# A three-stage attention and mixture kernel: the first mixture in blocks of 768 tokens, routing logits on TensorE, three token lists

## The chip, the core and the metric

The kernel runs on one core of a Trainium2 chip. Its engines work from queues of their own and meet through semaphores: TensorE multiplies (a weight load and a matmul each), VectorE and ScalarE read the accumulators in PSUM, GpSimd works on SBUF and issues the indirect DMAs, SyncE (SP) issues all other DMAs. The metric is the device time of one execution in microseconds (us), the median of several.

## The reference

What is computed, cut to its core (B=4, H=8, S=576, D=64, so 2304 tokens of 512 features; 8 experts, 1024 hidden features; float32 throughout):

```python
def phi(x):
    proj = np.einsum('bhsd,df->bhsf', x, w_phi)
    proj = proj - np.max(np.abs(proj), axis=-1, keepdims=True)
    return np.concatenate([np.exp(proj), np.exp(-proj)], axis=-1)
kv = einsum('bhsf,bhsd->bhfd', phi(k), v); z = sum(phi(k), axis=2)
x = einsum('bhsf,bhfd->bhsd', phi(q), kv) / (einsum('bhsf,bhf->bhs', phi(q), z)[..., None] + 1e-06)
# first mixture: every expert on every token, weighted by a Sinkhorn-normalised gate
P = np.exp(x @ w_gate - (x @ w_gate).max())
for _ in range(8):
    P /= P.sum(1, keepdims=True) + 1e-09
    P /= P.sum(0, keepdims=True) + 1e-09
    P *= N / E
x = sum(P[:, e:e + 1] * (np.maximum(x @ w1[e], 0.0) @ w2[e]) for e in range(E))
# second mixture: each token to the expert with the largest cosine logit
logits = (x / norm(x)) @ (emb / norm(emb)).T / tau
e = argmax(logits, axis=1); gate = softmax(logits)[e]
out[t] = gate[t] * (np.maximum(x[t] @ w1b[e[t]], 0.0) @ w2b[e[t]])
```

## The kernel before

Matrices are multiplied as float32r with a correction: each operand is split into a high part (a rounding copy, on ScalarE) and a low part (the difference, on VectorE or GpSimd), and each product is three matmuls, high by high, high by low, low by high.

**Attention** takes eight units (two batches by two heads), each in five chunks of keys and five of queries. Its output goes, transposed, to the DRAM tensor xd. While it runs, a background queue (`bg`) prepares the first expert's weights and the first block's activations, one task a step.

**First mixture.** The tokens are cut into four blocks of 512 and one of 256 (`BLOCKS`). For each expert and block there are two halves g of the hidden features. A half's first layer (`p1_group`) is a Winograd-Strassen scheme on 2 x 2 parts of the features and the tokens: seven products instead of eight, each of 12 matmuls of 256 columns, with adds on VectorE between them; `halves` then makes the relu's high part on ScalarE and its low part on VectorE. The 256-token block takes four plain products. The second layer (`p2_tile`) takes each tile of 128 tokens through 12 matmuls of 512 columns, and VectorE adds the result, weighted by the gate Pm, to an accumulator (acca, accb). Weights arrive in tiles called raw and go through `w1_tasks` (sums and splits, 11 operations a half, shared by VectorE and GpSimd) and `w2_task`. The block's activations are loaded again from xd in every step (`xload`), and their sums and splits made again (`x_tasks`, `xpiece`), by GpSimd and ScalarE.

The order is written out by hand: the instruction order of each engine is the order of the calls. `at_tick(step, g, i, fn)` puts a task behind a place of a step: the products of a half are its first ticks, the tiles of its second layer the next ones. `hooks` holds generators, of which one piece is issued at chosen ticks: `gate_logits` (gate products of a block, then the transposes) and `sinkhorn`, whose rounds alternate between VectorE and a matmul with ones (L676).

**Routing.** When the accumulators of a block are done, the second mixture's logits are made. For the first twelve tiles `dot_v` multiplies and sums a tile with an expert's embedding on VectorE (L749, four experts), `dot_p` and `dot_s` on GpSimd and ScalarE (the other four); for the last six `route_a` transposes a tile on TensorE and `route_l` multiplies it with the embeddings. `route_b` to `route_d` find each token's expert and its place in the expert's list with small VectorE operations and two matmuls; `route_w` writes the rows to the DRAM tensor x2d; `route_i` scatters the token numbers of one tile into the DRAM list ids with an indirect DMA, one tile after another into the same tensor:

```python
    def route_i(t0, i):
        si = rt[t0]["si"]
        G.indirect_dma_start(out=ids, out_offset=bass.IndirectOffsetOnAxis(si[:, i:i + 1], 0), in_=tokid[:, t0 + i:t0 + i + 1], in_offset=None)
```

**Second mixture.** 22 blocks of 128 list entries (25 if the counts need it), each of one expert. The first five (`NEARLY`) come from the first twelve tiles alone, so that they can start before the rest is routed. For each: `load_ids` reads the list, `gather` fetches the rows (tile xg), `tx` transposes them, `p1` and `p2` are the two layers, `th_` transposes the hidden rows in between; `wcond` loads an expert's weights when the expert changes, `wsplit` splits them. The output rows are scattered to their tokens.

## Time and profile before

| | |
|---|---|
| median of 3 runs | 2157.77 us (2156.74 to 2158.98) |
| the profiled execution's own time | 2161.89 us |
| its span, first to last instruction | 2160.0 us |
| mean granted TensorE clock | 0.979 |
| busy: TensorE, VectorE, ScalarE, GpSimd | 2052.9, 1289.6, 852.0, 886.1 us |
| moved by DMA | 148.78 MB, 69 GB/s in the mean |

The profile is of one execution, so durations and places below are of that one. Busy time of TensorE counts a matmul from its issue to its modelled end; consecutive matmuls overlap, so what one costs in a row of them is the distance of their starts, not its duration.

### The profile page before, as it was taken

The page shows a single profiled execution, that of the slowest core. Times are in us where ns is not written, and L with a number is a line of the kernel's source. Part 1 is how long each engine was busy: PE and PEld are TensorE (multiplying, and loading weights), DVE is VectorE, ACT ScalarE, POOL GpSimd, SP SyncE. Part 2 cuts the span into 40 slices and gives each one's busy share as a digit, 9 for nine tenths or more (in the row PEclk, how much of TensorE's full clock was granted, in tenths as well). Part 3 has the DMA queues.
Part 4 walks back from the last instruction along what each step waited for, and adds up shares of the span by engine and source line. Part 5 has one row for each costly group of instructions (what it writes and reads, how often), then busy time and mean ns, then how long its engine had stood idle before and what let it go on. Part 6 is the DMA issues. An engine that isn't in the chain of part 4 may idle for free.

```text
span 2160.0 us, 33113 instructions
## 1 busy us (share of the span) xinstructions
PE 2052.9 (95%) x12937; PEld 1839.7 (85%) x12937; DVE 1289.6 (60%) x1951; ACT 852.0 (39%) x1514; POOL 886.1 (41%) x678
## 2 busy tenths in 40 slices
PE   9999999999999999999999999999998886689997
PEld 8999889789989988898989899899987775568886
DVE  6776532764464464447446544744568784499996
ACT  5666422332342232224223222422334442468875
POOL 1234423343362344426224443532467662134442
PEclk9999999999999999999999999999999997889999
DMA  3443200111030012002100300310121013442851
GB/s 107 128 135 91 85 11 30 60 58 40 11 115 23 20 52 77 20 30 98 40 20 30 98 20 30 95 43 20 40 88 33 27 30 70 82 153 82 309 193 61
DMA packets 70674, 148.78 MB, mean 69 GB/s; under 512 B 10464, under 2 KB 30176, under 8 KB 70514
## 3 DMA queue, kind: packets, MB, share of 16 engines
q1 hardware_dynamic: 66418, 136.12, 19.8%
q0 software_dynamic: 4096, 10.51, 1.7%
q8 instruction: 103, 1.69, 0.3%
q14 instruction: 57, 0.47, 0.1%
HBM read 186.86 MB, written 15.32 MB: 94 GB/s over the span
## 4 chain that ended last, share of the span: by engine, by line
PE 67%; DVE 13%; issue 8%; DMA 5%; ACT 4%; POOL 3%; SPq 1%; POOLq 0%; DVEq 0%; ACTq 0%
PE psD L692 10%; PE psD L693 10%; PE psD L691 9%; PE psA L465 9%; PE psA L467 9%; PE psA L466 9%; PE psD L203 3%; DMA ids<-tokid,si 2%; DVE psB L749 2%; DMA xg<-x2d,idt 2%; DVE s2l L984 1%; PE psB L174 1%; DVE s1l L984 1%; PE psC L174 1%; DVE h1l L475 1%
## 5 line engine op out<-in xcount | busy, mean ns | idle before, releaser
L402 POOL TENSOR_TENSOR xlB<-xr,xhB 128x512 fp32r<-128x512 f32 x112 | 147.9, 1321 | 581.0 <-ACT xhB L401 578.8
L707 DVE SCALAR_TENSOR_TENSOR acca<-psD,Pm,acca 128x512 f32<-128x512 f32 x224 | 167.7, 749 | 237.6 <-PE psD L693 235.8
L691 PE MATMUL psD<-w2h,h1h 128*128 128x512 f32 x576 | 226.6, 393 | 7.6 <-ACT h1h L474 7.6
L691 PE MATMUL psD<-w2h,h0h 128*128 128x512 f32 x576 | 228.3, 396 | 3.1 <-DVE acca L707 3.1
L692 PE MATMUL psD<-w2h,h1l 128*128 128x512 f32 x576 | 227.0, 394 | 3.0 <-DVE h1l L475 3.0
L692 PE MATMUL psD<-w2h,h0l 128*128 128x512 f32 x576 | 225.7, 392 | 1.5 <-DVE h0l L475 1.4
L693 PE MATMUL psD<-w2l,h0h 128*128 128x512 f32 x576 | 226.3, 393 | 0.0
L693 PE MATMUL psD<-w2l,h1h 128*128 128x512 f32 x576 | 225.1, 391 | 0.1
L465 PE MATMUL psA<-xhT,wS 128*128 128x256 f32 x768 | 215.4, 280 | 0.0
L467 PE MATMUL psA<-xhT,wS 128*128 128x256 f32 x768 | 214.3, 279 | 0.0
L466 PE MATMUL psA<-xlT,wS 128*128 128x256 f32 x768 | 214.3, 279 | 0.0
L466 PE MATMUL psA<-xlB,wA 128*128 128x256 f32 x640 | 179.4, 280 | 4.1 <-POOL xlB L402 4.1
L465 PE MATMUL psA<-xhB,wA 128*128 128x256 f32 x640 | 180.6, 282 | 0.0
L467 PE MATMUL psA<-xhB,wA 128*128 128x256 f32 x640 | 179.4, 280 | 0.0
L495 ACT COPY tu<-psA 128x512 f32<-128x512 f32 x64 | 37.5, 586 | 350.7 <-PE psA L467 350.7
L467 PEld LDWEIGHTS psA<-xhT,wS 128*128 128x128 f32 x768 | 144.4, 188 | 0.0
L465 PEld LDWEIGHTS psA<-xhT,wS 128*128 128x128 f32 x768 | 144.2, 188 | 0.1
L466 PEld LDWEIGHTS psA<-xlT,wS 128*128 128x128 f32 x768 | 143.6, 187 | 0.0
L475 DVE SCALAR_TENSOR_TENSOR h0l<-psA,h0h 128x512 fp32r<-128x512 f32 x144 | 99.4, 690 | 65.4 <-ACT h0h L474 65.4
L984 DVE TENSOR_TENSOR s2l<-rw,s2h 128x1024 fp32r<-128x1024 f32 x88 | 115.7, 1363 | 37.6 <-POOL s2h L981 30.7
L691 PEld LDWEIGHTS psD<-w2h,h1h 128*128 128x128 f32 x576 | 108.9, 189 | 33.4 <-ACT h1h L474 10.7
L692 PEld LDWEIGHTS psD<-w2h,h1l 128*128 128x128 f32 x576 | 108.8, 189 | 31.9 <-DVE h1l L475 9.3
(299 smaller groups left out, 5679.5 us busy)
## 6 DMA issues: line engine op xcount, KB each, us to landing
rw<-in_moe_w SPq DMA_DIRECT2D x176, 512.0 KB
raw<-in_moe_w SPq DMA_DIRECT2D x64, 512.0 KB
xr<-xd SPq DMA_DIRECT2D x32, 1024.0 KB
v<-in_v SPq DMA_DIRECT2D x8, 715.0 KB
x2d<-acca SPq DMA_DIRECT2D x4, 1026.0 KB
rk<-in_kT SPq DMA_DIRECT2D x32, 128.0 KB
rq<-in_qT SPq DMA_DIRECT2D x32, 128.0 KB
xd<-xo SPq DMA_DIRECT2D x32, 128.0 KB
```

Source lines behind the costliest of these rows:

```text
L174: T.matmul(ps[:, sg, o:o + w], ek[:, 2 * ci + h_, sg, :], v[:, h_, s0 * W:s0 * W + w], start=(c == 0 and sg == 0), stop=(c == 8 and sg == 1))
L203: T.matmul(ps[:, off:off + w], eq[:, sg, h_, ci * P:(ci + 1) * P], kvz[:, h_, sg, o:o + w], start=(sg == 0), stop=(sg == 1))
L402: G.tensor_tensor(out=lo, in0=src, in1=f32(hi), op=ALU.subtract)
L465: T.matmul(bank[:, j, :], w[:, 0, j, k, :], xh[:, k, :], start=first, stop=False, skip_group_check=True)
L466: T.matmul(bank[:, j, :], w[:, 0, j, k, :], xl[:, k, :], start=False, stop=False, skip_group_check=True)
L467: T.matmul(bank[:, j, :], w[:, 1, j, k, :], xh[:, k, :], start=False, stop=end, skip_group_check=True)
L475: V.scalar_tensor_tensor(out=hl[:, :, ts_], in0=src, scalar=0.0, in1=f32(hh[:, :, ts_]), op0=ALU.max, op1=ALU.subtract)
L691: T.matmul(ps, hh[:, j, ts_], wh[:, ws], start=(hv == 0 and j == 0), stop=False)
L692: T.matmul(ps, hl[:, j, ts_], wh[:, ws], start=False, stop=False)
L693: T.matmul(ps, hh[:, j, ts_], wl[:, ws], start=False, stop=(hv == 1 and j == 1))
L707: V.scalar_tensor_tensor(out=o, in0=ps, scalar=Pm[:, t, e:e + 1], in1=o, op0=ALU.mult, op1=ALU.add)
L984: V.tensor_tensor(out=lo, in0=r, in1=f32(hi), op=ALU.subtract)
```

## The change

The first mixture takes three blocks of 768 tokens. A product of the first layer is done for one half j of the output features at a time, 6 matmuls of 384 columns, so a half g has 14 of them. The block order alternates from expert to expert, so the last block of one is the first of the next. The activation sums and splits are made in the first expert's steps alone and written to the DRAM tensor xpd; later steps load the seven pieces from there (`xreload`), each behind the last product that reads the old one. All sums and low parts of the weights go to GpSimd, in the ticks of the second layer (`w1_at`). Attention takes the second batch pair first. The gate's logits are made for each half of a block, with the transposes behind. Sinkhorn's hooks come at every odd tick.

Every tile is routed by `route_a` and `route_l`, in batches of three; the dot products on VectorE, GpSimd and ScalarE are gone. The i-th tile of a batch is scattered into the i-th of three lists, which begin with zeros; `load_ids` reads all three and `gather` adds them (on GpSimd) before the indirect DMA. Several tiles live elsewhere, and the calls at the start of the second mixture are in another order.

```diff
-BLOCKS = [(0, 512), (512, 512), (1024, 512), (1536, 512), (2048, 256)]
+TB = 768
+TH = TB // 2
+NB = NT // TB
+TPB = TB // P
+RB = 3
...
-    ids = dr.tile([NSLOT, 1], I32, name="ids")
+    ids = [dr.tile([NSLOT, 1], I32, name=f"ids{k}") for k in range(RB)]
     xd = dr.tile([P, KD, NT], F32, name="xd")
+    xpd = dr.tile([NB, len(XUSE), P, 2 * 2 * TH], F32, name="xpd")
     end = dr.tile([E, DM], F32, name="end")
...
-    units = [(bp, hp_) for bp in range(2) for hp_ in range(KD)]
+    units = [(bp, hp_) for bp in (1, 0) for hp_ in range(KD)]
...
-            V.tensor_tensor(out=a22, in0=a21, in1=a22, op=ALU.add)
+            G.tensor_tensor(out=a22, in0=a21, in1=a22, op=ALU.add)
...
+            wpiece(e, g, "S4", a12, G)
+            for _ in range(2):
                 load_next_w()
...
+    def xtile(name):
+        t = xk.tile([P, 2, 2, TH], F32R, tag="x" + name, name="x" + name)
+        xs[name] = t
+        return t
+
+    def quarter(kh, th, bi):
+        o = bi * TB + th * TH
+        return xd[:, 2 * kh:2 * kh + 2, o:o + TH]
+
+    def xstage(bi, q):
+        for t_, (kh, th) in zip(q, ((0, 0), (0, 1), (1, 1))):
+            SP.dma_start(out=t_, in_=quarter(kh, th, bi))
+
+    def xsplit(bi, name, src, eng):
+        t = xtile(name) if src is not None else xs[name]
+        src = f32(t[:, 1]) if src is None else src
+        A.copy(t[:, 0], src)
+        eng.tensor_tensor(out=t[:, 1], in0=src, in1=f32(t[:, 0]), op=ALU.subtract)
+        SP.dma_start(out=xpd[bi, XUSE.index(name)], in_=f32(t).rearrange("p l k t -> p (l k t)"))
+
+    def xdirect(bi, name):
+        t = xtile(name)
+        SP.dma_start(out=f32(t[:, 1]), in_=quarter(1, "B21 B22".split().index(name), bi))
...
+    def xreload(bi, n):
+        t = xtile(XUSE[n])
+        SP.dma_start(out=f32(t).rearrange("p l k t -> p (l k t)"), in_=xpd[bi, n])
+
+    XNEXT = ((0, 13, "load"), (1, 0, "T3a"), (1, 2, "T1a"), (1, 4, "T2a"), (1, 7, "B11"), (1, 8, "T2"), (1, 9, "T3"), (1, 10, "T1"), (1, 11, "B21d"), (1, 13, "B22d"), (1, 14, "T4a B21"), (1, 15, "T4 B22"))
+    XFIRST = ("T3a", "T1a", "T2a", "B11", "T2", "T3", "T1", "T4a", "B21", "T4", "B22")
+    ORDER = [(e, b_) for e in range(E) for b_ in ((2, 1, 0) if e % 2 == 0 else (0, 1, 2))]
+    NSTEP = len(ORDER)
...
+    def product(bank, g, j, wn, xn, start, stop):
         w = w1t[g, wn].rearrange("p l (j k f) -> p l j k f", j=2, k=2)
-        xh, xl = xs[xn]
...
+        x = xs[xn]
+        for k in range(2):
+            T.matmul(bank, w[:, 0, j, k, :], x[:, 0, k, :], start=start and k == 0, stop=False, skip_group_check=True)
+            T.matmul(bank, w[:, 0, j, k, :], x[:, 1, k, :], start=False, stop=False, skip_group_check=True)
+            T.matmul(bank, w[:, 1, j, k, :], x[:, 0, k, :], start=False, stop=stop and k == 1, skip_group_check=True)
...
+            hb[hv] = tuple(hp.tile([P, 2, TB], F32R, tag=f"h{hv}{q}", name=f"h{hv}{q}") for q in "hl")
+        for j in range(2):
+            b0 = psum("A", [P, TH])
+            product(b0, g, j, "A11", "B11", True, True)
+            tu = hp.tile([P, TH], F32, tag="tu", name="tu")
+            A.copy(tu, b0)
+            yield
+            b1 = psum("A", [P, TH])
+            product(b1, g, j, "S2", "T2", True, True)
+            add(tu, b1, tu)
+            yield
...
+            b3 = psum("A", [P, TH])
+            product(b3, g, j, "S1", "T1", True, True)
+            add(tv, b3, tv)
+            halves(1, j, 1, tv)
+            yield
+            product(b0, g, j, "A12", "B21", False, True)
+            halves(0, j, 0, b0)
+            yield
+            product(b2, g, j, "A22", "T4", False, True)
+            add(b2, b2, tu)
+            halves(1, j, 0, b2)
+            yield
+            product(b3, g, j, "S4", "B22", False, True)
+            add(b3, b3, tu)
+            halves(0, j, 1, b3)
+            yield
...
+        for th in range(2):
+            ps = psum("B", [2 * E, TH])
+            terms = ((0, "B11"), (1, "B21")) if th == 0 else ((2, "B22"), (3, "T3"))
+            for i, (j, nm) in enumerate(terms):
+                for kt in range(2):
+                    for l in range(2):
+                        T.matmul(ps, wgs[:, 2 * j + kt, :], xs[nm][:, l, kt, :], start=(i == 0 and kt == 0 and l == 0), stop=(i == 1 and kt == 1 and l == 1))
+            lt = acc(bi * TPB + 4 + th)[0:2 * E, 0:TH]
+            A.copy(lt, ps)
+            yield
+            nt, t0 = TH // P, bi * TPB + th * (TH // P)
+            pt = psum("C", [P, nt, 2 * E])
+            for t in range(nt):
+                T.transpose(pt[:, t, :], lt[:, t * P:(t + 1) * P], ident[0:2 * E, 0:2 * E])
+            V.tensor_copy(Pm[:, t0:t0 + nt, :], pt[:, :, 0:E])
+            V.tensor_tensor(out=Pm[:, t0:t0 + nt, :], in0=Pm[:, t0:t0 + nt, :], in1=pt[:, :, E:2 * E], op=ALU.add)
+            yield
...
     def load_ids(i):
         if i not in regs:
             load_regs(i)
+        idr[i] = c0.tile([P, RB], I32, tag="idr", bufs=5, name=f"idr{i}")
+        for k in range(RB):
+            SP.dma_start(out=idr[i][:, k:k + 1], in_=ids[k][bass.ds(regs[i][0], P), :])
+
+    def gather(i):
+        if not xgs:
+            xgs.append(wp.tile([P, 2, XW], F32, tag="wA11_0", name="xgs"))
+        r = idr.pop(i)
         idt[i] = c0.tile([P, 1], I32, tag="idt", bufs=5, name=f"idt{i}")
-        SP.dma_start(out=idt[i], in_=ids[bass.ds(regs[i][0], P), :])
-
-    def gather(i):
-        xg[i] = c0.tile([P, XW], F32, tag="xg", bufs=2, name=f"xg{i}")
+        G.tensor_tensor(out=r[:, 0:1], in0=r[:, 0:1], in1=r[:, 1:2], op=ALU.add)
+        G.tensor_tensor(out=r[:, 0:1], in0=r[:, 0:1], in1=ntok, op=ALU.add)
+        G.tensor_tensor(out=idt[i], in0=r[:, 0:1], in1=r[:, 2:3], op=ALU.add)
+        xg[i] = xgs[0][:, i % 2, :]
```

The schedule:

```diff
+    def w1_at(step, g, e, first_tick):
+        for i, fn in enumerate(w1_tasks(e, g)):
+            at_tick(step, g if e else 0, first_tick + i, fn)
+
...
+    w1_at(0, 1, 0, 13)
+    at_tick(0, 1, 4, w2_task(0, 1))
+    at_tick(0, 1, 8, w2_task(0, 3))
+    for step, (e, bi) in enumerate(ORDER):
+        nxt = ORDER[step + 1][1] if step + 1 < NSTEP else bi
+        if nxt != bi:
+            if e:
+                for n in range(len(XUSE)):
+                    at_tick(step, 1, 7 + n, partial(xreload, nxt, n))
+            else:
+                v_ = acca[:, 0:TPB, :].rearrange("p t w -> p (t w)")
+                q = [v_[:, 2 * TH * i:2 * TH * (i + 1)].rearrange("p (k t) -> p k t", k=2) for i in range(4)]
+                ops = x_tasks(nxt, q)
+                for g, i, ks in XNEXT:
+                    for k_ in ks.split():
+                        at_tick(step, g, i, ops[k_])
...
-            at_tick(step + 1, 0, f_ + 1, w2_task(e + 1, 3))
+        if step % NB == NB - 1 and e + 1 < E:
+            w1_at(step, 0, e + 1, 13)
+            at_tick(step, 1, 4, w2_task(e + 1, 0))
+            at_tick(step, 1, 8, w2_task(e + 1, 2))
+            w1_at(step, 1, e + 1, 13)
+            at_tick(step + 1, 0, 6, w2_task(e + 1, 1))
+            at_tick(step + 1, 0, 10, w2_task(e + 1, 3))
 
...
+    def route_at(step, t0, ticks):
+        for k, fn in route_steps(t0, *ticks):
+            at_tick(step, k // 20, k % 20, fn)
+
+    route_at(NSTEP - 2, 0, ((1, 2, 3), (3, 4, 5), (7, 11, 9, 12, 13, (13, 13, 13))))
+    route_at(NSTEP - 2, 3, ((6, 7, 8), (8, 9, 10), (14, 16, 15, 17, 18, (18, 18, 18))))
+    route_at(NSTEP - 1, 6, ((0, 1, 2), (2, 3, 4), (6, 10, 8, 11, 12, (12, 12, 12))))
+    route_at(NSTEP - 1, 9, ((4, 5, 6), (6, 7, 8), (12, 14, 13, 15, 15, (15, 15, 15))))
+    last = [(16, route_first)] + [(17, partial(load_ids, i)) for i in range(NEARLY)]
+    last += [(18, partial(gather, 0)), (18, partial(load_raws, 2, (0, 1))), (19, partial(gather, 1)), (29, partial(load_raws, 2, (2,))), (33, start_second)]
+    last += [(34 + c, partial(first_w1, 0, (c,))) for c in range(4)] + [(35, partial(tx, 0)), (38, partial(tx, 1)), (38, partial(first_w1, 1, (0, 1))), (39, partial(first_w1, 1, (2,)))]
+    tail = route_steps(NA, (36, 37, 38), (37, 38, 39), (40, 41, 41, 41, 41, (41, 41, 41)))
+    last += tail[:6]
+    for k, fn in last:
+        at_tick(NSTEP - 1, k // 20, k % 20, fn)
```

## Rows read from the trace of the kernel before

**Rows 1.** The table of stretches of the whole core, by time windows that end at the places named in the prediction. Columns: the stretch in us from the span's start and its length, then busy us (and instructions) of TensorE, its weight loads, VectorE, ScalarE and GpSimd, the granted TensorE clock as a share of full speed, the mean busy share of the 16 DMA engines and the GB/s that they moved.

```profile
0.00:202.50 202.50, 197.90 (x1714) 195.46 (x1715) 138.47 (x325) 122.22 (x295) 66.51 (x98) 0.99 0.38 116
202.50:423.40 220.90, 215.88 (x1412) 192.85 (x1411) 104.66 (x182) 74.64 (x135) 74.86 (x56) 1.00 0.15 49
423.40:1577.10 1153.70, 1140.84 (x7212) 1030.63 (x7211) 606.03 (x813) 342.89 (x582) 484.06 (x347) 1.00 0.14 47
1577.10:1838.90 261.80, 213.41 (x1267) 189.49 (x1265) 181.61 (x330) 95.96 (x218) 149.27 (x109) 0.91 0.20 53
1838.90:2150.40 311.50, 284.89 (x1341) 231.24 (x1339) 258.85 (x304) 215.60 (x286) 110.42 (x69) 0.95 0.46 149
2150.40:2160.00 9.60, 0.00 (x0) 0.00 (x0) 0.00 (x0) 0.69 (x1) 0.98 (x1) 0.77 0.03 11
```

**Rows 2.** The timeline of TensorE in one steady step of the first mixture, expert 4. Columns: start us, duration us, engine, line, operation, output<-inputs. The first row begins the 84 matmuls of one half of a 512-token block's first layer, the second the 48 of its second layer, the third the next half.

```profile
1027.63 0.28 PE L465 MATMUL psA<-xhB,wA 128*128 128x256 f32 x1
...
1037.53 0.40 PE L691 MATMUL psD<-w2h,h0h 128*128 128x512 f32 x1
...
1048.44 0.28 PE L465 MATMUL psA<-xhB,wA 128*128 128x256 f32 x1
```

**Rows 3.** The chain of waits that ended last, in order of time. Columns: start us, us, what. Two places one expert apart, and between them the piece at the turn from one expert to the next.

```profile
995.89 1.36 issue
...
1005.93 2.84 POOL w2l L388
...
1187.05 1.36 issue
```

**Rows 4.** The list of who waited for whom over the whole span. Columns: the waiting engine, output and line <- what it waited for: us in total, times, longest us.

```profile
POOL ids L853 <- DMA ids<-tokid,si: 73.6, 13, 9.4
...
PE psA L465 <- DVE tv L479: 24.4, 6, 6.8
...
PE psD L1046 <- DVE hTl L1030: 19.1, 3, 15.4
...
PE psA L992 <- DMA xg<-x2d,idt: 16.4, 5, 14.2
```

**Rows 5.** The view of one tensor, the token list ids: how long its scatters took from issue to landing.

```profile
DMA to landing us min/median/max: 4.7/7.8/10.1
```

**Rows 6.** Groups of instructions of VectorE and ScalarE, by line and tile. Columns: line, engine, operation, output<-inputs, output<-input shapes, count | busy us, mean ns of one | idle us before them and what ended it.

```profile
L475 DVE SCALAR_TENSOR_TENSOR h0l<-psA,h0h 128x512 fp32r<-128x512 f32 x144 | 99.4, 690 | 65.4 <-ACT h0h L474 65.4
L479 DVE TENSOR_TENSOR psA<-psA,tu 128x512 f32<-128x512 f32 x128 | 88.8, 693 | 3.1 <-PE psA L467 1.4
...
L475 DVE SCALAR_TENSOR_TENSOR h1l<-tv,h1h 128x512 fp32r<-128x512 f32 x64 | 48.4, 757 | 49.3 <-ACT h1h L474 49.3
...
L672 DVE TENSOR_TENSOR Pm<-Pm,rs 128x144 f32<-128x144 f32 x8 | 6.0, 753 | 0.3
L679 DVE TENSOR_TENSOR Pm<-Pm,cs 128x144 f32<-128x144 f32 x8 | 4.2, 526 | 0.3
L670 DVE TENSOR_SCALAR rs<-rs 128x18 f32<-128x18 f32 x8 | 3.5, 435 | 0.3
L673 DVE TENSOR_REDUCE cs<-Pm 128x8 f32<-128x144 f32 x8 | 3.4, 422 | 0.3
...
L474 ACT ACTIVATE h0h<-psA 128x512 fp32r<-128x512 f32 x144 | 86.1, 598 | 112.6 <-DVE psA L479 60.1 <-PE psA L467 44.3 <-PE psB L817 5.8
...
L495 ACT COPY tu<-psA 128x512 f32<-128x512 f32 x64 | 37.5, 586 | 350.7 <-PE psA L467 350.7
...
L232 ACT COPY xo<-psA 128x256 f32<-128x256 f32 (+1 forms) x34 | 11.6, 342 | 5.0 <-ACT ek L159 4.9
```

**Rows 7.** Two windows of 10 us in the second mixture, columns as in rows 1, while expert weights are loaded.

```profile
2020.00:2030.00 10.00, 10.00 (x49) 8.19 (x48) 10.00 (x12) 7.74 (x10) 2.37 (x2) 1.00 0.98 351
2040.00:2050.00 10.00, 9.86 (x50) 7.97 (x49) 8.06 (x10) 7.62 (x11) 6.51 (x3) 1.00 1.01 379
```

**Rows 8.** Groups of GpSimd, columns as in rows 6.

```profile
L402 POOL TENSOR_TENSOR xlB<-xr,xhB 128x512 fp32r<-128x512 f32 x112 | 147.9, 1321 | 581.0 <-ACT xhB L401 578.8 <-PE psD L188 2.1
...
L331 POOL TENSOR_TENSOR wA<-raw,wA 128x512 fp32r<-128x512 f32 x32 | 49.8, 1571 | 119.5 <-ACT wA L330 119.4
...
L388 POOL TENSOR_TENSOR w2l<-raw,w2h 128x1024 fp32r<-128x1024 f32 x8 | 22.7, 2837 | 16.6 <-ACT w2h L384 16.6
```

**Rows 9.** One group of TensorE, columns as in rows 6: the matmul that sums a Sinkhorn column over the partitions.

```profile
L676 PE MATMUL psC<-cs,ones 128*128 128x8 f32 x16 | 2.7, 238 | 5.0 <-DVE cs L673 5.0
```

**Rows 10.** The timeline of TensorE where the fourth batch of tokens is routed, columns as in rows 2: four transposes of one tile, eight small matmuls of two tiles.

```profile
1794.31 1.05 PE L771 MATMUL psB<-ident,acca 128*128 128x128 f32 x4
...
1797.45 0.95 PE L781 MATMUL psC<-enT,scr 128*128 128x8 f32 x8
```

**Rows 11.** The timeline of TensorE in the second mixture, columns as in rows 2: the first matmul of two blocks that are five blocks apart.

```profile
1968.95 0.48 PE L1013 MATMUL psA<-s1h,xth 128*128 128x512 f32 x1
...
2030.67 0.48 PE L1013 MATMUL psA<-s1h,xth 128*128 128x512 f32 x1
```

**Rows 12.** The timeline of GpSimd there, columns as in rows 2, with the idle time before the instruction and what ended it: two gathers.

```profile
2001.34 1.72 POOL L958 DMA_INDIRECT xg<-x2d,idt  x1 [6.25 <-PE psD L1046]
...
2028.13 3.27 POOL L958 DMA_INDIRECT xg<-x2d,idt  x1 [7.63 <-DMA idt<-ids]
```

**Rows 13.** The view of one tile, xg, from 1990 to 2100 us: how long its gathers took from issue to landing.

```profile
DMA to landing us min/median/max: 6.6/7.6/8.7
```

463 lines of the change are left out of this document (132 added, 331 removed).

## The prediction

> **What bounds the kernel now.** I read the stage table first [rows 1]: stretches cut at the first matmul of the first mixture (202.5 us), of its expert 1 (423.4), of its expert 7 (1577.1) and of the second mixture (1838.9), and at the last matmul (2150.4). The reader is to see TensorE's busy time against each stretch: nearly without a break up to 1577.1, at a granted clock of 0.99 to 1.00; 48 us short in the stretch of expert 7 (213.4 of 261.8, clock 0.91), 27 us short in the second mixture (0.95). So up to 1577.1 only fewer or cheaper matmuls help; after that, shorter waits do.
>
> Busy time hides the price of one matmul, because they overlap. Starts show it [rows 2]: 84 matmuls of 256 columns take from 1027.63 to 1037.53, 9.90 us, 117.9 ns each; 48 of 512 columns from there to 1048.44, 10.91 us, 227.3 ns each. One expert is 768 of the first and 432 of the second: 90.5 + 98.2 = 188.7 us. The chain of waits gives the period, 1187.05 - 995.89 = 191.2 us [rows 3], so a steady expert loses 2.5 us, at the turn to the next one, where the chain runs through GpSimd's split of w2 (2.84 us). The waits [rows 4] name the rest: TensorE waits on VectorE ahead of products (24.4 us in six waits, up to 6.8), once 14.2 us for a gathered tile, 15.4 us for the hidden layer's low half. Behind the last two stands GpSimd, which waits 73.6 us, 13 times, for its previous scatter into the one token list; a scatter lands after 7.8 us in the median [rows 5].
>
> **1. Blocks of 768.** Seven products of 12 matmuls become, in each of three blocks, two times seven of 6, with 384 columns: 4032 matmuls for 6144. The trace has no 384. The line through 256 and 512 gives 172.6 ns; the 512 price per column gives 170.5, the 256 price 176.8. I take the line, since nothing shows a step between. 6144 x 0.1179 = 724.4 becomes 4032 x 0.1726 = 695.9: 28.5 us less, 3.5 an expert (bounds 12 to 37). An expert is then 87.0 + 98.2 = 185.2 us.
>
> The rows differ here from the Trainium skill ("TensorE: Matmul & The Clock Gate", section "Back-to-back issue gap"), which gives a warm start-to-start of the columns over 2.4 GHz plus 2.5 ns: 162.5 ns for 384 columns, 109.2 for 256. By it the gain would be an estimated 15.7 us, not 28.5; the trace has 117.9 and 227.3 where the page has 109.2 and 215.8, so the measurement decides.
>
> Does the shorter product still hide the chain of VectorE and ScalarE behind it? A 512-wide VectorE step is 0.69 us, an activation 0.60; a 256-wide copy is 0.34 against 0.59 for 512 [rows 6], so 384 columns should take about 0.56 and 0.47. A set of seven products holds 5 adds and 4 low halves, 5.1 us, and three waits for ScalarE, 1.7 us: 6.8 of its 7.25 us. VectorE runs 2.7 us late at the end of a set, and the fourth product of the next, which needs that bank, starts after 3.1. Hidden, with 0.4 us to spare and little room for anything added.
>
> **2. Activation sums in DRAM.** Expert 0 makes the sums once and writes them (21 pieces of 786 KB); experts 1 to 7 reload seven pieces at two turns each, 98 loads through SP's queue. Removed: 40 loads of x, and most of GpSimd's and ScalarE's work on it. A reload goes out when its piece's last product ends: the first 8.3 us into a half of 30.9, needed at its end; the seventh is needed 28.8 us after the first issue. Bursts of weights run at 351 to 379 GB/s [rows 7]: 5.5 MB in 15 to 16 us. Hidden, no cost; if late, TensorE itself would wait.
>
> **3. Weight splits on GpSimd.** Eleven operations of 1.3 to 1.6 us [rows 8] and its waits for ScalarE's casts, about 18 us, start with the 16.4 us of output matmuls and end 2 us into the next half, which needs other tiles. The last one that ScalarE's queue waits for is over before the first product. The turn's 2.5 us go; I keep 0.5 an expert. In the attention stage four casts now wait behind GpSimd: nothing to 6 us, taken 2. In expert 0, GpSimd makes the weights of half two and the next block's sums together: eight 768-wide operations of 2 us, three half-made sums, two w2 splits of 2.84. Laid end to end it is 2.2 us late for w2 and on the edge for the last sums: 4 us (0 to 12).
>
> **4. Sinkhorn and gate.** The hooks now come every second product. A pair of them brings VectorE four operations of 0.42 to 0.75 us [rows 6] and four that I estimate at 0.2 to 0.3, 3.0 us, into 4.1 us that were 93% full: 2.7 us of TensorE waiting for each of some six pairs that fall among products, 16 us, 11 of them in expert 0. Before, the wait rows have 5.0 us on the reduction [rows 9], and experts 1 to 6 hold 1153.7 - 6 x 191.2 = 6.5 us over their period. Net: +6.5 in expert 0, and 5.5 kept in expert 1 (bounds -4 and +8 together). The gate's transposes are placed otherwise: nothing.
>
> **5. Routing on TensorE.** VectorE's and GpSimd's dot products go. Each of 12 more tiles brings 4 transposes and 4 small matmuls. Eight of the latter span 0.95 us [rows 10]; I take 0.11 us for each of both, 0.88 a tile. Expert 7 holds 15 tiles: 13.2 us, and 0.8 of input transposes. ScalarE's square and copy (1.2 us a tile by [rows 6]) and the small VectorE chains fall among products that have no room: two chains at 3 us, one at 1.5, four groups of tiles at 2 each, 15 us together (0 to 35). Expert 7: 185.2 + 14.0 + 15 = 214.2.
>
> **6. Three lists.** Three scatters of a batch go to three tensors, so only batches follow each other, and these are several products apart: the 73.6 us go. The first gathers are issued some 40 us ahead of the second mixture. Against it stand 66 id loads on SP's queue for 22, and three small additions on GpSimd ahead of each gather, behind which its casts and output scatters queue. A block of the second mixture takes (2030.67 - 1968.95) / 5 = 12.34 us [rows 11]. A gather issued at 2001.34 [rows 12] lands 7.6 us later [rows 13], at 2008.9; it is wanted after the first layer of the block that starts at 1968.95 + 3 x 12.34 = 2005.97, some 24 x 0.23 = 5.5 us on, with 2 to 3 us left. Where weights are loaded the gather goes out at 2028.13, 2.5 us before its block, and there nothing is left. The additions have no row; from under 0.1 us to 0.6 each. I take 8 us in all (2 to 38). Second mixture: 22 x 12.34 = 271.5, 2.7 for the last three tiles, 6 for their waits on ScalarE (0 to 15), 8: 288.2.
>
> **Sum.** 202.5 + 2 = 204.5; 220.9 - 3.5 + 4 + 6.5 = 227.9; six experts of 185.7 and 5.5 = 1119.7; 214.2; 288.2; the end 9.6 [rows 1]. Together 2064.1 for a span of 2160.0: 96 us less. The profiled execution took 2161.9 us for that span, 4 more than the median of 2157.8; from the median it is **2062 us**.
>
> **Rivals.**
> - *Routing is no cheaper (0.12).* Every transpose waits for ScalarE's copy of the tile before, through one bank. For: the clock of 0.91 in that stretch, and ScalarE in order. Against: its load there falls with the x casts. Expert 7 stays near 262: 2062 + 48 = 2110.
> - *GpSimd sets the pace of weights (0.12).* At 1.57 us an operation [rows 8] and 3 us more of waits, ScalarE's queue blocks the next half's relus, 3 us at two places in seven turns: +42, 2104. Against: in experts 1 to 6 GpSimd is busy 42% [rows 1], and x work leaves it. The Trainium skill ("SBUF — State Buffer", section "SBUF: two separate sides") has VectorE with two SBUF inputs and GpSimd reading SBUF lock each other out for a whole instruction. The trace agrees as far as it goes: the low half that reads tv takes 757 ns, those that read PSUM 690 [rows 6].
> - *The additions show in every block (0.09).* 2 us in 19 blocks: 30 over the 8 taken, 2092.
> - *Slower (0.05): reloads come late.* At each of 14 turns TensorE would wait for the seventh piece. It decides when a turn loses 96 / 14 = 6.9 us, so when 5.5 MB take over 35.7 us, under 154 GB/s; at 110 GB/s a turn takes 50 us, 14 x 21 = 297 us, 2359. For: these stretches move 47 GB/s now [rows 1], and SP issues in order behind weight loads. Against: [rows 7].
> - *No change (0.02):* several of these together.
>
> The forecast holds with 0.60. Around it go the price of 384 columns (-8, +16), expert 7 (-15, +20), expert 0 and Sinkhorn (-8, +10). The range, **2035 to 2108**, takes in these, the second and third rival and about half of the first. Runs of this kernel spread by 0.1%, so 0.2% is what can be told from no change. Faster 0.93, same 0.02, slower 0.05.
>
> **What would show it.** Starts of 384-column matmuls 0.170 to 0.177 us apart; a period of 185 to 187 us an expert; no wait of TensorE for a piece's DMA; 10 to 20 us of waits on Sinkhorn's reduction; expert 7 in about 214 us at a clock over 0.95; GpSimd's waits for scatters under 15 us; a second mixture of about 288. It would be wrong if x pieces or GpSimd's weights appear as releasers in the steady experts, or if a 384-column matmul costs more than 177 ns.

## The result, and the profile after

The changed kernel takes 2095.33 us in the median of 4 runs (2091.79 to 2097.44), against 2157.93 us of the kernel before: a ratio of 0.9708, 95% interval 0.9691 to 0.9726. It is faster, inside the range, and 33 us above the forecast of 2062. The profiled execution took 2091.79 us for a span of 2089.7; the experiments below ran on other chips, where the kernel before takes 2165 to 2167 us and the changed kernel, taken again on one of them, 2096.05, a ratio of 0.9681 (0.9656 to 0.9705). Variants are therefore compared by their ratio to the kernel before on their own chip; a difference in us below is one of medians, some of them of two chips, and good to a few us.

The table of stretches of the kernel after, cut at the same places as [rows 1] and with the same columns:

```profile
0.00:205.90 205.90, 200.16 (x1713) 197.96 (x1714) 132.71 (x318) 123.85 (x295) 77.74 (x105) 0.98 0.42 132
205.90:424.70 218.80, 214.91 (x1131) 187.87 (x1130) 101.97 (x219) 75.59 (x142) 98.26 (x63) 1.00 0.30 107
424.70:1557.90 1133.20, 1130.76 (x5621) 1015.63 (x5620) 508.16 (x880) 249.95 (x486) 225.62 (x157) 1.00 0.22 81
1557.90:1772.30 214.40, 210.59 (x1134) 188.76 (x1132) 108.30 (x258) 57.99 (x121) 26.17 (x28) 1.00 0.46 91
1772.30:2080.40 308.10, 287.77 (x1355) 232.56 (x1354) 251.67 (x320) 215.90 (x288) 154.48 (x131) 0.97 0.45 149
2080.40:2089.70 9.30, 0.04 (x1) 0.00 (x0) 0.00 (x0) 0.69 (x1) 0.97 (x1) 0.63 0.03 11
```

Against the sum of the prediction:

| stretch | before | predicted | after | missed by |
|---|---|---|---|---|
| attention | 202.5 | 204.5 | 205.9 | +1.4 |
| expert 0 | 220.9 | 227.9 | 218.8 | -9.1 |
| experts 1 to 6 | 1153.7 | 1119.7 | 1133.2 | +13.5 |
| expert 7 | 261.8 | 214.2 | 214.4 | +0.2 |
| second mixture | 311.5 | 288.2 | 308.1 | +19.9 |
| end | 9.6 | 9.6 | 9.3 | -0.3 |

That is 25.6 us of span. The other 7.6 are a matter of which execution: before, the profiled one lay 4 us above its median, after, 3.5 below.

The steady step of expert 4, TensorE's timeline as in [rows 2]: first matmul of a half's first layer, of its second layer, of the next half.

```profile
993.13 0.34 PE L443 MATMUL psA<-xB,wA 128*128 128x384 f32 x1
...
1007.84 0.39 PE L666 MATMUL psD<-w2h,h0h 128*128 128x512 f32 x1
...
1024.57 0.34 PE L443 MATMUL psA<-xB,wA 128*128 128x384 f32 x1
```

84 matmuls of 384 columns take 14.71 us, 175.1 ns each (173.5 in the other halves). But 72 of 512 columns take 16.73 us, 232.4 ns each, where [rows 2] have 227.3 for the same operation. The first of these stretches as a row with the columns of [rows 1]:

```profile
993.13:1007.84 14.71, 14.71 (x85) 14.71 (x84) 8.10 (x15) 6.19 (x11) 4.40 (x3) 1.00 0.29 89
```

The waits, columns as in [rows 4]:

```profile
POOL idr L894 <- DMA idr<-ids: 108.6, 18, 16.2
...
PE psA L932 <- DMA xgs<-x2d,idt: 9.6, 9, 2.6
...
POOL ids L784 <- DMA ids<-tokid,si: 8.7, 3, 4.7
...
PE psA L953 <- DVE gt L938: 7.2, 1, 7.2
...
PE psC L651 <- DVE cs L648: 5.7, 5, 1.3
...
PE psB L711 <- DVE sl L764: 2.6, 1, 2.6
```

GpSimd's 73.6 us behind scatters are 8.7. In their place stand 108.6 us behind id loads, and TensorE waits nine times for gathered rows. No activation piece and no weight split is among TensorE's waits in the steady experts.

The second mixture's opening, one window of 30 us with the columns of [rows 1]:

```profile
1800.00:1830.00 30.00, 21.38 (x89) 16.36 (x88) 29.25 (x53) 20.70 (x27) 16.18 (x15) 0.83 0.28 62
```

VectorE is busy 29.25 of 30 us here, TensorE 21.38, at a granted clock of 0.83: this is where the wait of 7.2 us lies. The clock falls during it: TensorE is busy 4.70 us of the stretch from 1810 to 1820, and from 1820 to 1830 the granted clock is 0.65, which is 70% of the time at the lower of its two levels. The four blocks of the opening still take 64 us (1772.34 to 1836.45) where they took 80 before (1838.87 to 1919.18); the blocks behind them give most of that back.

### The profile page after: what moved, and what is told of

Its sections match the earlier page's. It is cut to its first block, busy times and chain, and to the rows that moved or that the text cites. A ratio compares the mean times of both kernels' runs of the same rounds, so it can differ in the third digit from the quotient of the medians.

```text
span 2089.7 us, 28848 instructions
## 1 busy us (share of the span) xinstructions
PE 2044.2 (98%) x10947; PEld 1822.8 (87%) x10947; DVE 1102.8 (53%) x1994; ACT 724.0 (35%) x1331; POOL 583.2 (28%) x482
## 4 chain that ended last, share of the span: by engine, by line
PE 82%; DVE 5%; DMA 3%; POOL 3%; issue 3%; ACT 2%; SPq 1%; POOLq 0%; DVEq 0%; ACTq 0%
PE psD L666 13%; PE psD L667 13%; PE psD L668 13%; PE psA L443 11%; PE psA L444 11%; PE psA L445 11%; PE psD L197 3%; DMA idr<-ids 1%; DVE s2l L924 1%; PE psB L168 1%; PE psC L168 1%; POOL xgs L898 1%; DVE s1l L924 1%; DMA rw<-in_moe_w 1%; PE psD L182 1%
## 5 line engine op out<-in xcount | busy, mean ns | idle before, releaser
L327 POOL TENSOR_TENSOR wA<-raw,wA 128x512 fp32r<-128x512 f32 x48 | 60.9, 1298 | 817.1 <-ACT wA L326 817.0
L667 PE MATMUL psD<-w2h,h0l 128*128 128x512 f32 x576 | 227.2, 395 | 0.6 <-DVE h0l L453 0.6
L668 PE MATMUL psD<-w2l,h0h 128*128 128x512 f32 x576 | 227.2, 395 | 0.0
L668 PE MATMUL psD<-w2l,h1h 128*128 128x512 f32 x576 | 227.2, 394 | 0.0
L443 PE MATMUL psA<-xT,wS 128*128 128x384 f32 x576 | 195.7, 340 | 0.0
L445 PE MATMUL psA<-xT,wS 128*128 128x384 f32 x576 | 194.1, 337 | 0.0
L444 PE MATMUL psA<-xT,wS 128*128 128x384 f32 x576 | 194.0, 337 | 0.0
L452 ACT ACTIVATE h1h<-tv 128x384 fp32r<-128x384 f32 x96 | 50.3, 524 | 265.5 <-DVE tv L457 265.5
L453 DVE SCALAR_TENSOR_TENSOR h0l<-psA,h0h 128x384 fp32r<-128x384 f32 x192 | 106.4, 554 | 62.2 <-ACT h0h L452 61.8
L677 DVE SCALAR_TENSOR_TENSOR accb<-psD,Pm,accb 128x512 f32<-128x512 f32 x84 | 63.1, 751 | 137.2 <-PE psD L668 125.7
L452 ACT ACTIVATE h0h<-psA 128x384 fp32r<-128x384 f32 x192 | 94.2, 491 | 112.9 <-DVE psA L457 105.9
L668 PEld LDWEIGHTS psD<-w2l,h1h 128*128 128x128 f32 x576 | 108.6, 188 | 25.5
L668 PEld LDWEIGHTS psD<-w2l,h0h 128*128 128x128 f32 x576 | 108.5, 188 | 25.2
L443 PE MATMUL psA<-xB,wA 128*128 128x384 f32 x384 | 130.2, 339 | 0.0
L666 PEld LDWEIGHTS psD<-w2h,h0h 128*128 128x128 f32 x576 | 108.5, 188 | 24.1 <-DVE accb L677 1.0
```

The lines of the kernel that those rows point to most:

```text
L327: eng.tensor_tensor(out=t[:, 1], in0=src, in1=f32(t[:, 0]), op=ALU.subtract)
L443: T.matmul(bank, w[:, 0, j, k, :], x[:, 0, k, :], start=start and k == 0, stop=False, skip_group_check=True)
L444: T.matmul(bank, w[:, 0, j, k, :], x[:, 1, k, :], start=False, stop=False, skip_group_check=True)
L445: T.matmul(bank, w[:, 1, j, k, :], x[:, 0, k, :], start=False, stop=stop and k == 1, skip_group_check=True)
L452: A.activation(out=hh[:, j, ts_], in_=src, func=AF.Relu)
L453: V.scalar_tensor_tensor(out=hl[:, j, ts_], in0=src, scalar=0.0, in1=f32(hh[:, j, ts_]), op0=ALU.max, op1=ALU.subtract)
```

## The experiments

**1 and 2. Where the 5 ns of a 512-column matmul come from.** The first idea was the place of the hidden layer, the stationary operand, which the change moved to the other side of the on-chip memory.

```diff
-    hp = top.enter_context(tc.tile_pool(name="hp", bufs=1, side="right"))
+    hp = top.enter_context(tc.tile_pool(name="hp", bufs=1))
```

> The changed kernel with one tile pool moved: the hidden layer's tiles (h0h, h0l, h1h, h1l, tu, tv, the stationary operands of the second layer) lie again on the left side of the on-chip memory, as in the kernel before, where a 512-column matmul of the second layer took 227.3 ns; in the changed kernel they lie on the right side, at high addresses, and it takes 232.4. Theory A (the place of the stationary operand sets the price): 227.3 ns again, 24 blocks x 144 matmuls x 5.1 ns = 17.6 us less, 2078 us, and the second mixture's second layer, whose stationary tiles stay on the right, stays at 232. Theory B (the 5 ns come from something else of the change, such as the 1536-byte rows, the reloads or the new order): no change, 2095 us, within 4.

Ratio 0.9683 (0.9658 to 0.9707), the changed kernel's own. A 512-column matmul of the second layer takes 233.3 ns. Theory A falls. The other idea was alignment:

```diff
+    rpad = top.enter_context(tc.tile_pool(name="rpad", bufs=1, side="right"))
+    pad = rpad.tile([P, 24], F32, name="pad")
+    G.memset(pad, 0.0)
     hp = top.enter_context(tc.tile_pool(name="hp", bufs=1, side="right"))
```

> The changed kernel with 96 bytes of padding ahead of all tiles on the right side of the on-chip memory, so that they begin at multiples of 128 bytes instead of 96 bytes beyond one; they stay at high addresses. Theory A (it is the side or the height of the address): the second layer's matmuls stay at 232.4 ns, 2095 us within 4. Theory B (it is the alignment of the stationary operand): 227.3 ns, both mixtures, 17.6 + 22 x 48 x 5.1 ns = 23 us less, 2072 us.

Ratio 0.9692 (0.9672 to 0.9712), 233.2 ns: alignment of the stationary operand alone does nothing either, and "it is the side" had fallen with the first run. Both theories were too narrow, so I laid the start of every matmul in the traces beside the byte addresses of its two operands in the compiled program:

| kernel, matmuls | stationary, mod 512 | moving, mod 512 | median from start to start, ns |
|---|---|---|---|
| before, second layer, 512 columns | 416 | 416 | 227 |
| before, second mixture's first layer | 480 | 480 / 416 | 227 / 233 |
| after, second layer | 480 | 96 | 232 |
| after, second mixture's first layer | 480 | 480 / 64 | 227 / 232 |
| run 1, second layer | 64 | 96 | 234 |
| run 2, second layer | 384 | 96 | 233 |
| before, first layer, 256 columns | 416 | 480 | 118 |
| after, first layer, 384 columns | 64 | 480 | 174 |

Where the offsets agree, 227; where not, 232 to 234, within one kernel too. The kernel before had agreeing offsets in its second layer; the change shifted its tiles.

**3. All operands at one offset.** 320 bytes ahead of the right side; the gate column leaves the accumulators' rows, so that their sizes are multiples of 512.

```diff
-    acca = m1.tile([P, NA, XW], F32, name="acca")
-    accb = accp.tile([P, NTL - NA, XW], F32, name="accb")
+    acca = m1.tile([P, NA, DM], F32, name="acca")
+    accb = accp.tile([P, NTL - NA, DM], F32, name="accb")
+    gcol = c0.tile([P, NTL], F32, name="gcol")
...
-        V.reciprocal(rows[:, :, DM], se)
-        SP.dma_start(out=x2d[t0 * P:(t0 + n) * P, :].rearrange("(t p) d -> p t d", p=P), in_=rows)
+        V.reciprocal(gcol[:, t0:t0 + n], se)
+        x2r = x2d[t0 * P:(t0 + n) * P, :].rearrange("(t p) d -> p t d", p=P)
+        SP.dma_start(out=x2r[:, :, 0:DM], in_=rows)
+        SP.dma_start(out=x2r[:, :, DM], in_=gcol[:, t0:t0 + n])
```

> The changed kernel with every tile of matmul operands (weights, activations, hidden layer, both mixtures) at the same byte offset modulo 512, namely 160: 320 bytes of padding ahead of the right side, and the gate column moved out of the accumulators' rows into a tile of its own (one small DMA more for each batch of tokens). In the traces so far every group of 512-column matmuls whose two operands lie at one offset modulo 512 started 227 ns apart, every other 231 to 233. Theory A (the two operands' relative offset sets the price): the second layer of the first mixture at 227.3 instead of 232.4 (3456 x 5.1 ns = 17.6 us), of the second mixture too (2.7 us and 1 us in its first layer), and perhaps the 384-column products at 170.5 instead of 174.3, the 512 price by columns (15 us more): ratio to the changed kernel 0.983 to 0.990. Theory B (the agreement is chance): 232 to 233 again, no change within 0.2%.

The changed kernel beside it, on the same chip:

> The changed kernel itself, to have it on the same chip as the variants beside it: the ratio to the kernel before stays 0.971 within 0.002.

Ratio 0.9560 (0.9543 to 0.9577) against 0.9681: 23.5 us less by the medians. TensorE's timeline in expert 4, as above:

```profile
985.19 0.34 PE L446 MATMUL psA<-xB,wA 128*128 128x384 f32 x1
...
999.79 0.39 PE L670 MATMUL psD<-w2h,h0h 128*128 128x512 f32 x1
...
1016.15 0.33 PE L446 MATMUL psA<-xB,wA 128*128 128x384 f32 x1
```

72 matmuls in 16.36 us, 227.2 ns. The 384-column products stay at 173.8 (14.60 us for 84), so that part of theory A fails: the offset moves them by no more than 1 ns. One expert now takes 185.8 us; the prediction had 185.7, with 0.5 for a pause that did not come and 0.6 too little for 384 columns. (One weight tile of 14 remained 32 bytes off.)

**4. The kernel before with one offset everywhere.** The same edit of its gate column.

> The kernel before, with the gate column in a tile of its own, by which all its operand tiles come to one offset modulo 512 (480); until now its first layer's weights lay at 416 and its activations at 480, its second layer's operands both at 416. Theory A (relative offset): the second layer stays at 227.3 ns; the 256-column products, 117.9 ns, fall to about 113.7 (half of 227.3), 6144 x 4.2 ns = 26 us less, 0.988 of the kernel before, and its second mixture's first layer goes from 231 to 233 (three of four weight pieces) to 227. Theory B: no matmul price moves and the time stays within 0.2%.

Ratio 1.0045 (1.0028 to 1.0062): slower, by some 10 us. The timeline of TensorE, columns as in [rows 2]:

```profile
1029.20 0.28 PE L465 MATMUL psA<-xhB,wA 128*128 128x256 f32 x1
...
1039.28 0.40 PE L692 MATMUL psD<-w2h,h0h 128*128 128x512 f32 x1
...
1050.18 0.28 PE L465 MATMUL psA<-xhB,wA 128*128 128x256 f32 x1
```

84 matmuls of 256 columns take 10.08 us, 120.0 ns, not 113.7: with equal offsets they cost 2 ns more than the 117.9 of [rows 2]; 6144 of them are 12.9 us. The 512-column ones stay (227.1), and some 200 of the second mixture's first layer that stood at 233 now stand at 227. So theory A holds for 512 columns, and its extension by columns is wrong in sign.

**5. The token lists undone.** (Tile idt also has seven buffers instead of five here.)

```diff
-    ids = [dr.tile([NSLOT, 1], I32, name=f"ids{k}") for k in range(RB)]
+    ids = dr.tile([NSLOT, 1], I32, name="ids")
...
-        for k in range(RB):
-            SP.dma_start(out=idr[i][:, k:k + 1], in_=ids[k][bass.ds(regs[i][0], P), :])
+        SP.dma_start(out=idt[i], in_=ids[bass.ds(regs[i][0], P), :])
...
-        G.tensor_tensor(out=r[:, 0:1], in0=r[:, 0:1], in1=r[:, 1:2], op=ALU.add)
-        G.tensor_tensor(out=r[:, 0:1], in0=r[:, 0:1], in1=ntok, op=ALU.add)
-        G.tensor_tensor(out=idt[i], in0=r[:, 0:1], in1=r[:, 2:3], op=ALU.add)
```

> The changed kernel without its three lists: all tiles of a batch scatter into one list again, 22 id loads instead of 66, and no additions ahead of a gather. Theory A (the lists are what shortens the gap ahead of the second mixture): GpSimd waits for scatters again, 12 to 15 times and 60 to 100 us, the first gathers come some 20 us later than their transposes on TensorE, and the last six scatters push on the blocks after them; the additions' cost goes: 2110 to 2130 us. Theory B (three lists bring nothing once routing is on TensorE, since the batches lie far enough apart, and the additions cost 10 us or more): 2080 to 2095 us.

Ratio 0.9836 (0.9819 to 0.9853), 35 us over the changed kernel by the medians, so theory A, beyond its upper end. A wait, and the stretches of expert 7 and of the second mixture:

```profile
POOL ids L783 <- DMA ids<-tokid,si: 98.6, 14, 8.7
```

```profile
1558.90:1806.90 248.00, 220.43 (x1134) 196.00 (x1134) 108.34 (x258) 58.03 (x121) 25.80 (x22) 0.93 0.36 79
1806.90:2120.50 313.60, 289.30 (x1355) 235.26 (x1354) 264.07 (x320) 215.02 (x287) 93.46 (x70) 0.95 0.46 146
```

Expert 7 takes 248.0 us again instead of 214.4. What TensorE waits for there, and the reason in GpSimd's and VectorE's timelines:

```profile
PE psD L665 <- DVE acca L676: 11.1, 1, 11.1
PE psD L665 <- DVE accb L676: 10.2, 1, 10.2
```

```profile
1751.54 0.96 POOL L783 DMA_INDIRECT ids<-tokid,si  x1 [7.17 <-DMA ids<-tokid,si]
1752.52 0.88 POOL L726 TENSOR_TENSOR ss<-ss,half 128x3 f32<-128x3 f32 x1
```

```profile
1753.44 0.17 DVE L753 TENSOR_SCALAR ss<-ss 128x3 f32<-128x3 f32 x1 [10.11 <-POOL ss L726]
```

GpSimd makes the norms ss of the next batch (L726) behind scatters of the last one, VectorE stands 10.11 us for them, and TensorE for the accumulators that VectorE has still to clear. The first gather goes out at 1786.68, behind six scatters from 1738.15 on. The other side shows in the second mixture: its last 17 intervals between blocks take 12.41 us each with one list (1890.77 to 2101.68) and 13.25 with three, 14 us in all. That is what the id loads and additions cost there.

**6. The lists alone, in the kernel before.** Four lists for its batches of four, three additions.

```diff
-    ids = dr.tile([NSLOT, 1], I32, name="ids")
+    ids = [dr.tile([NSLOT, 1], I32, name=f"ids{k}") for k in range(4)]
...
-        G.indirect_dma_start(out=ids, out_offset=bass.IndirectOffsetOnAxis(si[:, i:i + 1], 0), in_=tokid[:, t0 + i:t0 + i + 1], in_offset=None)
+        G.indirect_dma_start(out=ids[i], out_offset=bass.IndirectOffsetOnAxis(si[:, i:i + 1], 0), in_=tokid[:, t0 + i:t0 + i + 1], in_offset=None)
```

> The kernel before with the lists alone: each of the four tiles of a batch scatters into a list of its own, and a block's ids are four loads and three additions on GpSimd; routing, blocks and all else as before. Theory A (the single list is what holds up the opening of the second mixture: GpSimd waits 73.6 us in 13 for scatters, TensorE 14.2 us for a gathered tile and 15.4 us for a hidden layer's low half behind it): these waits go and the time falls by 15 to 30 us, 0.986 to 0.993 of the kernel before. Theory B (the lists help only where routing on TensorE has freed the other engines): within 0.3% of the kernel before, or slower by the later ids.

Ratio 0.9932 (0.9912 to 0.9952), 16 us by the medians: theory A, at its weak end. Stretches, then waits:

```profile
1574.80:1817.50 242.70, 209.78 (x1267) 185.42 (x1265) 178.95 (x329) 94.76 (x216) 150.05 (x115) 0.94 0.21 53
1817.50:2138.80 321.30, 287.91 (x1341) 233.38 (x1339) 248.37 (x304) 217.65 (x287) 155.70 (x130) 0.95 0.45 148
```

```profile
POOL idt L964 <- DMA idt<-ids: 115.9, 19, 18.3
...
PE psA L1001 <- DMA xg<-x2d,idt: 19.2, 12, 4.1
```

Expert 7 gains 19.1 us and the second mixture gives 9.8 back, behind late ids: GpSimd's wait is now for them, and TensorE's waits for gathered rows are 19.2 us in twelve where they were 16.4 in five. Runs 5 and 6 make a square for the stretch of expert 7: 261.8 with neither, 242.7 with the lists, 248.0 with everything but the lists, 214.4 with both. The two effects, 19 for the lists and 14 for the rest of the change, sum to 33; together they bring 47. Which part of the rest it is, the routing or another, no run separates.

**7. Ids four blocks ahead.**

```diff
-            if i + 2 >= NEARLY and i + 2 < i1:
-                load_ids(i + 2)
+            ahead = 2 if i0 else 4
+            if i > NEARLY - 3 and i + ahead < i1:
+                load_ids(i + ahead)
...
                 for _ in ob:
                     pass
+                load_ids(NEARLY)
+                load_ids(NEARLY + 1)
```

> The changed kernel with the id loads of the second mixture issued four blocks ahead instead of two, so that on SP's queue they no longer stand just behind the weight loads of the same block. Theory A (GpSimd's additions and the gather behind them are late because the ids are): GpSimd's waits for ids, 92.5 us in 17 in the second mixture, fall under 25 us, TensorE's waits for gathered rows, 9.6 us in 9, under 3 us, and the time falls by 7 to 14 us, to 2081 to 2088. Theory B (VectorE, 97% busy in the opening and 80% after it, sets the pace of the blocks, and the gathers are only late with it): under 3 us, 2092 to 2097.

Ratio 0.9632 (0.9599 to 0.9665), 12.7 us under the changed kernel by the medians, 10.6 by the ratios; its four runs lie between 2077.24 and 2093.79. Waits and the second mixture:

```profile
POOL idr L894 <- DMA idr<-ids: 27.1, 3, 14.2
...
PE psA L932 <- DMA xgs<-x2d,idt: 2.0, 2, 1.3
```

```profile
1769.50:2066.20 296.70, 282.99 (x1355) 230.89 (x1354) 261.48 (x320) 214.66 (x287) 134.09 (x130) 0.98 0.47 155
```

308.1 has become 296.7, with the additions still there: theory A. An interval between the later blocks is 12.67 us, where three lists had 13.25 and one list 12.41, so in these profiles the late ids are 10 of the 14 us and the additions the other 4. What hurt was that the loads came late; whether by the weight loads ahead of them in SP's queue or by a lead of only two blocks is not shown, since the edit changes both. What follows a late id, GpSimd's and VectorE's timelines of the changed kernel show:

```profile
1899.46 0.19 POOL L894 TENSOR_TENSOR idr<-idr 128x1 int32<-128x1 int32 x1 [4.85 <-DMA idr<-ids]
1899.73 0.19 POOL L895 TENSOR_TENSOR idr<-idr,ntok 128x1 int32<-128x1 int32 x1
1899.99 3.58 POOL L896 TENSOR_TENSOR idt<-idr 128x1 int32<-128x1 int32 x1
1903.85 0.99 POOL L898 DMA_INDIRECT xgs<-x2d,idt  x1 [0.27 <-POOL idt L896]
```

```profile
1900.04 3.48 DVE L924 TENSOR_TENSOR s2l<-rw,s2h 128x1024 fp32r<-128x1024 f32 x3
```

An addition that takes 0.19 us alone takes 3.58 when it starts just ahead of three splits of VectorE, 3.48 us in a row, and the gather waits. That is the rule which the prediction named from the Trainium skill ("SBUF — State Buffer", section "SBUF: two separate sides"): VectorE with two SBUF inputs and GpSimd reading SBUF lock each other out. This trace agrees that one of the two stands still while the other works, and for a whole row of instructions instead of one. It does not show that the first to start goes first, as the Trainium skill has it there: by the profile the addition began 0.05 us ahead of the splits.

**8. Both repairs together.** The edits of runs 3 and 7.

> The changed kernel with the same offsets and with the id loads four blocks ahead, both together. Theory A (two independent losses): the gains add up: 18 to 36 us of the offsets and 12 to 16 us of the ids, ratio to the kernel before 0.946 to 0.957. Theory B (the offsets do nothing): the gain of the ids alone, 0.963 to 0.965.

2059.02 us, ratio 0.9497 (0.9479 to 0.9514), better than both kernels. Run 3 took 2072.53, run 7 2083.39; against the changed kernel's 2096.05 the gains of 23.5 and 12.7 sum to 36.2, and 37.0 came: theory A. Runs 3 and 8 lie on one chip and their times do not overlap, so the ids' 13.5 us there are surer than run 7's.

**9. The same, 64 bytes apart.** The one edit that changes nothing but the relative offset:

```diff
-    pad = rpad.tile([P, 80], F32, name="pad")
+    pad = rpad.tile([P, 64], F32, name="pad")
```

> The version with the same offsets and the ids ahead, with 64 bytes less of padding ahead of the right side and nothing else changed: activations, hidden layer and the second mixture's stationary tiles now lie at 224 modulo 512, weights still at 160. Theory A (the relative offset sets the price): 512-column matmuls go back from 227.4 to 232 or 233 ns in the second layers of both mixtures and in most of the second mixture's first layer, (3456 + 528 + 200) x 5.1 to 5.8 ns = 21 to 24 us more; the 384-column products, which cost about as much at every offset so far (173.3 to 175.1), may move by 1 ns, 4 us. Ratio to the kernel before 0.957 to 0.963 where that version had 0.950. Theory B (it was the gate column's move out of the accumulators): no change, 0.948 to 0.952.

Ratio 0.9646 (0.9630 to 0.9662), 2090.04 us: 31 us more. Second layers at 233.3 and 233.2 ns, and the second mixture's first layer at 227 where both operands lie at 224 and at 233 where the weights lie at 160. Theory A. Of the 31 us, 24 are this price; in its profile expert 0 took 226.8 us instead of 216.8, 2.6 by the price and the rest mostly a wait of 5.9 us for a low half of the hidden layer. Why that came is open.

**10. Weight splits on VectorE again.**

```diff
-            wpiece(e, g, "A11", a11, G)
+            wpiece(e, g, "A11", a11, V)
...
-            G.tensor_tensor(out=a22, in0=a21, in1=a22, op=ALU.add)
+            V.tensor_tensor(out=a22, in0=a21, in1=a22, op=ALU.add)
...
-            (V if e == 0 and c == 0 else G).tensor_tensor(out=lo, in0=r, in1=f32(hi), op=ALU.subtract)
+            (G if c == 2 else V).tensor_tensor(out=lo, in0=r, in1=f32(hi), op=ALU.subtract)
```

> The changed kernel with the weights' sums and low parts shared as in the kernel before: five of eleven operations a half, and three of four low parts of the second layer's weights, on VectorE instead of GpSimd, at the same places of the order. Theory A (the engine: taking the splits from VectorE is what closed the pause of 2.5 us at the turn from one expert to the next): the pause comes back, 1 to 2.5 us at each of seven turns, 7 to 17 us more than the changed kernel. Theory B (the place: in blocks of 768 these operations lie beside 16.7 us of second-layer matmuls, where VectorE is busy some 5 us): within 3 us of the changed kernel, no wait of TensorE at the turns.

Ratio 0.9784 (0.9768 to 0.9800), 22 us more by the medians, 12 to 18 by the profiled spans (2107.3 against 2094.9 and 2089.7). Experts 1 to 6, and TensorE's waits:

```profile
429.20:1575.00 1145.80, 1137.24 (x5622) 1014.46 (x5621) 599.12 (x982) 249.81 (x486) 80.74 (x54) 1.00 0.22 81
```

```profile
PE psD L667 <- DVE h0l L453: 4.8, 8, 0.6
...
PE psA L443 <- DVE h0l L453: 1.9, 7, 0.3
PE psA L443 <- DVE tv L457: 1.8, 2, 1.6
PE psA L443 <- DVE h1l L453: 1.8, 7, 0.3
```

The steady period goes from 188.3 to 190.5 us (813.08 to 1003.57) and waits for VectorE's halves and sums appear, three of them seven or eight times, about once an expert: theory A, at or over its upper end. It is not the old pause again, though: a lateness of a few tenths at four places, 10.3 us in all, makes most of the 12.6 us that experts 1 to 6 lose, and expert 0 loses 4.4 more.

**11. Four splits of the opening to GpSimd,** in the version of run 8.

```diff
-        V.tensor_tensor(out=lo, in0=r, in1=f32(hi), op=ALU.subtract)
+        eng = G if (which, i, c) in ((1, 2, 1), (2, 1, 1), (1, 3, 1), (1, 3, 3)) else V
+        eng.tensor_tensor(out=lo, in0=r, in1=f32(hi), op=ALU.subtract)
```

> The version with the same offsets and the ids ahead, with four of the low parts of the weights of the second mixture's blocks 1 to 3 (1.2 us each on VectorE) given to GpSimd. Theory A (VectorE's queue sets the opening of the second mixture, where TensorE waits 7.2 us for the fourth block's rows to be split and 2.6 us for slots): these waits fall by 4 to 7 us in all and the time with them, to 2052 to 2056 where that version took 2059. Theory B (GpSimd, at 2 to 3 us an operation, delays a gather or a scatter by as much): within 3 us of it or slower.

Ratio 0.9543 (0.9527 to 0.9559), 7 us slower than run 8, though its profiled span is the same (2060.6 and 2060.2). The waits:

```profile
PE psD L993 <- DVE s2l L931: 3.7, 1, 3.7
PE psA L960 <- DVE gt L945: 3.0, 1, 3.0
...
PE psD L993 <- POOL s2l L931: 1.5, 1, 1.5
```

The wait for gt falls from 7.2 to 3.0 us, and 5.2 us for split weights take its place: theory B. With the two engines' work shared, the opening is no shorter; what would shorten it stays open.

## Why the prediction was right, and where it missed

- **Faster, and mostly where forecast.** Expert 7 gives 47.4 us (forecast 47.6), so the rival that routing is no cheaper fell; experts 1 to 6 give 20.5 (forecast 34.0). Expert 7's 214.2 met 214.4 by luck, by cancelling terms: the matmul prices added 3.1, so of 15 us for busy engines 2.9 were too many. Of the signs, the 384-column price, the reloads, the scatters and expert 7 at a clock of 1.00 came; the period (188.3 against 185 to 187), Sinkhorn's waits (5.7 against 10 to 20) and the second mixture did not. No run undoes the blocks of 768, the reload or the routing alone; that they work as forecast is read from the trace after.
- **Step 1 missed its biggest term.** 384 columns at 172.6 ns against 173.5 and 175.1 measured lies inside its bounds; 4032 x 1.7 ns are 6.9 us. But the 98.2 us an expert, 432 matmuls of 512 columns at 227.3, were kept without asking what the price depends on. 3456 matmuls at 5.1 ns are 17.6 us, 13.2 of them in experts 1 to 6, and 2.7 us more in the second mixture. [Rows 2] could not show it; the 231 to 233 ns in the first layer of the old second mixture, which the prediction rounded to 0.23 us, could have.
- **Step 2, the reload, was right:** no wait for a piece in any of 14 turns, so the slower rival fell. So did the one of GpSimd's pace: no product waits for a weight split.
- **Step 3 was right about the turn:** the pause went (0.5 us kept, none found). Run 10 shows that VectorE, given these splits again, costs about as much at other places; that the old pause itself was VectorE's load is not shown, since its chain ran through GpSimd [rows 3]. Its 4 us in expert 0, and step 4's 12 us for Sinkhorn, were too high. All of Sinkhorn's waits on its reduction are 5.7 us in the span, and expert 0 came in 9.1 under the sum, 12.2 without the matmul prices. The two allowances there are 10.5; where the other 1.7 went is open. My reckoning, "3.0 us, into 4.1 us that were 93% full", did not hold: it counted VectorE's waits for ScalarE as filled. VectorE is busy 8.10 of the 14.71 us of a steady first layer, so it has room between for Sinkhorn, and TensorE's longest wait for a reduction is 1.3 us, not 2.7.
- **Step 6 had the right object and the wrong size.** 8 us for late gathers. From the fifth block on a block takes 13.25 us in the mean (1836.45 to 2061.68, 17 blocks) where [rows 11] have 12.34: 15 us, of which 2 are the price. The five blocks of [rows 11] were smooth ones; over these 17 the kernel before took 12.50 (1919.18 to 2131.68), so 3 us were there already. Run 7 takes 10 back. I priced the additions' durations and not three loads that come late. The rival "additions show in every block" (2092) gave nearly the time that came, but by luck: it puts 38 us (30 over the 8) on what is 14 by run 5, most of it late ids, and has none of the 27 us of matmul prices.
- **The opening was not in the sum.** From 1772.34 to 1836.45 TensorE holds four first and three second layers, 43.2 us by [rows 11], and my allowances of 8.7 us: 12.2 us are missing, where VectorE was busy 29.25 of 30 us and the granted clock fell. Six tiles are routed there while the list of the later blocks is made and weights are split. That VectorE's load is the cause is argued, not shown: run 11 took four splits from it and the opening stayed as long.

Together: 20.3 for 512 columns, 6.9 for 384, 11.8 for the opening without its share of the price, 5.4 for the later blocks beyond price and allowance, 1.1 at both ends; less 20.0 of allowances not spent (12.2 in expert 0, 2.9 in expert 7, 1.9 for Sinkhorn in expert 1, 3.0 at the turns of experts 1 to 6). That is 25.5, of 25.6 us; the allowances are found by subtraction, so the agreement proves little. Some 45 us that the sum did not have met 20 that it had too many: that the time came no further from 2062 is in part luck.

## What to carry to other kernels

A price read from the trace belongs to the addresses it was read at: when a change moves tiles, look at the start-to-start time of a matmul that the change does not touch, first of all. Price a small operation by when its input arrives and what waits behind it, not by its duration: here three small loads that came late cost more than the additions they fed. Count an engine's waits as room, not as work. And two halves of a remedy, like the lists and the rest of this change, can be worth more together than their sum, so an ablation of either alone misleads.
